# A cross network on one core: the first layer's second half column-tiled, its remainder transposed by DMA

## The chip, the cores and the metric

The kernel runs on one core of a Trainium2 chip. The metric is the device time of one execution in microseconds; lower is better. Before the change it is 131.33 us, the median of 3 runs (131.24 to 131.58).

## The reference

```python
B, F, D, L = 4096, 26, 16, 6
Din = min(F * D, 1024)                 # 416
# x0: (4096, 416), ws: (6, 416, 416), bs: (6, 416), all bf16
def reference(x0, ws, bs):
    x = x0
    for l in range(ws.shape[0]):
        x = x0 * (x @ ws[l] + bs[l]) + x
    return x
```

Six layers, each a product of 4096 rows with a 416 x 416 matrix, a bias, a multiplication with the first input and an addition.

## The kernel before, in words

The width of 416 is 3 x 128 + 32: three main blocks (`NK`) and a remainder of 32 (`R`). Through the first five layers the data lie transposed, features on the partitions. `XM` holds the three main blocks of all 4096 rows of the batch. `XR` holds the remainder, four groups of 512 rows stacked on the partitions, 32 partitions each. The batch is cut into two halves `s` of 2048 rows, each half into four quarters `g` of 512 rows (`CW`). A quarter of a half is written (s, g) here.

There are three shapes of product on the matmul engine (PE). A full product uses the array's 128 x 128 (L214 in the first layer, L327 in the last). A column-tiled group is four products of 128 x 32 that fill the array together (`mm_full`, L181; the remainder's, L193 and L198). A row-tiled group is four products of 32 x 128, the remainder's rows into the main blocks (L187, L221, L333).

The PSUM pool has four tiles of two banks under one tag, so every new tile waits for the release of an older one. ACT adds the bias and moves PSUM to SBUF (L165, L173). DVE multiplies by x0 and adds x (L166, L169, L174, L175).

The first layer (`first_layer(s)`) runs as the input arrives. SP issues a transposing load for each quarter (`load_x0t`, L76): four for half 0, (1,0), then `xrem` (the remainder columns of half 1, in rows, L85), then (1,1) to (1,3), then the weights of later layers (`load_wm`, `load_wr`), the rows of x0 for the last layer (`X0rows`) and the last bias. GpSimd (POOL) rearranges `xrem` into `xrig[:, 1]` (L134), between two fills of the block weights `WD` (`fill_wd`, L131). PE transposes four tiles of `xrig` with the identity (`x0_rem`, L157), for half 0 among its products, for half 1 at the end of half 0; DVE copies the result into `XR[0]` and, with the two halves of the partitions exchanged, into `XRd` (L160). `XRd` is the source of the row tiles of block 1 (L221).

Within a half the products are: the first two quarters for each block m into `pa[m]` (`full`), the row tiles of these and of `pb[0]`, the last two quarters into `pb[m]`, the row tiles of `pb[1]` and `pb[2]`, and the remainder's products (`mm_rem`, 16 products in four groups) into `pr`. Then follow the bias and the elementwise work for `pb` and `pr`.

Layers 1 to 4 run in the column-tiled shape, with the remainder of both halves in one `rem_pair`. The last layer turns the product round, so that rows of the batch come out on the partitions (`mm_q_full`, L327, 416 columns): eight blocks of 128 rows a round, in four rounds. Its elementwise work ends the kernel.

`tc.keep_in_program_order` pins an instruction behind those before it on its engine; the others the scheduler may move.

Of the kernel before, what the change touches and what calls it, by code (L numbers as in the profile page):

```python
# [11 lines left out]
BF16 = mybir.dt.bfloat16  # L12
FP32 = mybir.dt.float32
# [3 lines left out]
def kernel(  # L17
# [7 lines left out]
    nc = tc.nc  # L25
    B, D = x0.shape
    L = ws.shape[0]
    P = 128
    NK = 3
# [38 lines left out]
    def col0(s, g):  # L68
        return SW * s + CW * g

    def load_wm(eng, l):
        eng.dma_start(WM[:, l], ws[l, 0:NK * P, :].rearrange("(k p) n -> p k n", p=P))

    def load_x0t(s, g):
        c0 = col0(s, g)
        nc.sync.dma_start_transpose(out=XM[0][:, :, c0:c0 + CW], in_=x0[c0:c0 + CW, 0:NK * P])  # L76
# [35 lines left out]
            nc.gpsimd.tensor_copy(dst, src)  # L112
    for g in range(2, NG):
        load_x0t(0, g)
    load_x0t(1, 0)
    load_xrem1()
    for g in range(1, NG):
        load_x0t(1, g)
    load_wm(nc.sync, 1)
    for g in range(NG):  # L120
        load_wr(nc.sync, g, 1, L)
# [7 lines left out]
    def fill_wd(l0, l1):  # L129
        for g in range(NG):  # L130
            nc.gpsimd.tensor_copy(WD[32 * g:32 * g + 32, l0:l1, g, :], WR[32 * g:32 * g + 32, l0:l1, NK * P:D])  # L131

    fill_wd(0, 1)
    nc.gpsimd.tensor_copy(xrig[:, 1].rearrange("p i (g r) -> p i g r", g=NG), xrem[:].rearrange("p (g i) r -> p i g r", g=NG))  # L134
    fill_wd(1, L)

    wps = psum.tile([P, CW], FP32, tag="ps", name="wps")

# [7 lines left out]
    def bias_setup():  # L146
        pb = psum.tile([P, 4, 8], BF16, tag="ps", name="pb")
        for m in range(NK):
            nc.tensor.transpose(pb[:, m, 0:L], bsb[0:L, 128 * m:128 * m + 128], ident[0:L, 0:L])
        for g in range(NG):  # L150
            nc.tensor.transpose(pb[32 * g:32 * g + 32, 3, 0:L], bsb[0:L, NK * P:D], ident[0:L, 0:L], tile_position=(0, 32 * g))  # L151
        nc.vector.tensor_copy(bM[:], pb[:, 0:NK, 0:L])  # L152
        nc.vector.tensor_copy(bR[:], pb[:, 3, 0:L])

    def x0_rem(s, tpr):
        for i in range(4):
            nc.tensor.transpose(tpr[:, 128 * i:128 * i + 128], xrig[:, s, i, :], ident[:])  # L157
        for dst, src in ((slice(0, P), slice(0, P)), (slice(64, P), slice(0, 64)), (slice(0, 64), slice(64, P))):
            to = XR[0] if dst == src else XRd
            nc.vector.tensor_copy(to[dst, CW * s:CW * s + CW], tpr[src])  # L160

    def ew_main(l, s, m, h, pt, cur, nxt, pin=False):
        c0 = col0(s, 2 * h)
        t = tpool.tile([P, 2 * CW], BF16, name="t")
        nc.scalar.activation(t[:], pt[:].rearrange("p a b -> p (a b)"), ACT.Identity, bias=bM[:, m, l:l + 1], scale=1.0)  # L165
        prod = nc.vector.tensor_tensor(out=t[:], in0=t[:], in1=XM[0][:, m, c0:c0 + 2 * CW], op=ALU.mult)  # L166
        if pin:
            tc.keep_in_program_order(prod)
        nc.vector.tensor_tensor(out=nxt[:, m, c0:c0 + 2 * CW], in0=t[:], in1=cur[:, m, c0:c0 + 2 * CW], op=ALU.add)  # L169

    def ew_rem(l, s, pr, curR, nxtR):
        tr = tpool.tile([P, 2 * CW], BF16, name="t")
        nc.scalar.activation(tr[:, 0:CW], pr, ACT.Identity, bias=bR[:, l:l + 1], scale=1.0)  # L173
        nc.vector.tensor_tensor(out=tr[:, 0:CW], in0=tr[:, 0:CW], in1=XR[0][:, CW * s:CW * s + CW], op=ALU.mult)  # L174
        nc.vector.tensor_tensor(out=nxtR[:, CW * s:CW * s + CW], in0=tr[:, 0:CW], in1=curR[:, CW * s:CW * s + CW], op=ALU.add)  # L175
# [15 lines left out]
    def mm_rem(l, s, pr, cur, curR):  # L191
        for g in range(NG):
            nc.tensor.matmul(pr[32 * g:32 * g + 32, :], lhsT=WD[:, l, g, :], rhs=curR[:, CW * s:CW * s + CW],  # L193
                             start=True, stop=False, tile_position=(0, 32 * g))
        for k in range(NK):
            for g in range(NG):
                c0 = col0(s, g)
                nc.tensor.matmul(pr[32 * g:32 * g + 32, :], lhsT=WM[:, l, k, NK * P:D], rhs=cur[:, k, c0:c0 + CW],  # L198
                      start=False, stop=(k == NK - 1), tile_position=(0, 32 * g))
# [4 lines left out]
    def xl_dmat(s, k, nxt):  # L204
        nc.sync.dma_start_transpose(out=XLrows[:, 16 * s:16 * s + 16, 128 * k:128 * k + 128],
                                    in_=nxt[:, k, SW * s:SW * s + SW])

    def first_layer(s):
        cur, curR, nxt, nxtR = XM[0], XR[0], XM[1], XR[1]

        def full(pt, m, h, gl, after_row):
            c0 = col0(s, 2 * h + gl)
            for k in range(NK):
                nc.tensor.matmul(pt[:, gl, :], lhsT=WM[:, 0, k, 128 * m:128 * m + 128], rhs=cur[:, k, c0:c0 + CW],  # L214
                                 start=(k == 0 and not after_row), stop=(k == NK - 1 and after_row))

        def row(pt, m, h, opens):
            for gl in range(2):
                rg = 32 * ((2 * h + gl) ^ (2 if m == 1 else 0))
                src = XRd if m == 1 else curR  # L220
                nc.tensor.matmul(pt[:, gl, :], lhsT=WR[rg:rg + 32, 0, 128 * m:128 * m + 128],  # L221
                                 rhs=src[rg:rg + 32, CW * s:CW * s + CW],
                                 start=opens, stop=not opens, tile_position=(rg, 0))

        def ph(m):
            return psum.tile([P, 2, CW], FP32, tag="ps", name=f"ph{m}")

        pa = [ph(m) for m in range(NK)]
        if s == 0:
            for m in range(NK):  # L230
                full(pa[m], m, 0, 0, False)
            tp0 = psum.tile([P, CW], BF16, tag="ps", name="tpr")
            x0_rem(0, tp0[:])
            for m in range(NK):
                full(pa[m], m, 0, 1, False)
        else:
            for m in range(NK):
                for gl in range(2):
                    full(pa[m], m, 0, gl, False)
        pb = [ph(0)]  # L240
        row(pa[0], 0, 0, False)
        row(pb[0], 0, 1, True)
        row(pa[2], 2, 0, False)
        row(pa[1], 1, 0, False)
        for m in range(NK):
            ew_main(0, s, m, 0, pa[m], cur, nxt)
        for m in range(NK):
            if m:
                pb.append(ph(m))
            for gl in range(2):  # L250
                full(pb[m], m, 1, gl, m == 0)
        row(pb[1], 1, 1, False)
        row(pb[2], 2, 1, False)
        pr = psum.tile([P, 2, CW], FP32, tag="ps", name="pr")
        mm_rem(0, s, pr[:, 0, :], cur, curR)
        if s == 0:
            x0_rem(1, pr[:, 1, :].bitcast(BF16)[:, 0:CW])
        for m in range(NK):
            ew_main(0, s, m, 1, pb[m], cur, nxt, pin=(s == 0))
        ew_rem(0, s, pr[:, 0, :], curR, nxtR)  # L260

    bias_setup()
    pe_filler(1, CW)
    for s in range(NS):
        first_layer(s)

    def rem_pair(l, cur, curR, nxtR, feeds_last):
        pr2 = psum.tile([P, 2, CW], FP32, tag="ps", name="pr2")
        for s in range(NS):
            mm_rem(l, s, pr2[:, s, :], cur, curR)  # L270
        for s in range(NS):
            ew_rem(l, s, pr2[:, s, :], curR, nxtR)
            if feeds_last:
                nc.sync.dma_start_transpose(out=scrR[s][:], in_=nxtR[:, CW * s:CW * s + CW])

    def xl_rem(s):
        tc.keep_in_program_order(
# [42 lines left out]
    def q_cols(q, g):  # L320
        s, i = quads[q]
        c = col0(s, g) + 128 * i
        return slice(c, c + 128)

    def mm_q_full(q, g, py, closes):
        for k in range(NK):
            nc.tensor.matmul(py[:, 0:D], lhsT=cur[:, k, q_cols(q, g)], rhs=WM[:, l, k, :],  # L327
                             start=((not closes) and k == 0), stop=(closes and k == NK - 1))

# [33 lines left out]
    for q, at, done in rounds:  # L363
        tiles = [psum.tile([P, 2, CW], FP32, tag="ps", name=f"py{n}") for n in range(4)]
        bank = [tiles[n][:, a, :] for n, a in at]

        def close(u, n):
            tl, a = at[u]
            ew(q + u // 4, u % 4, n, tiles[tl][:, a:a + n, 0:D], nc.scalar if q + 2 == NQ and u == 7 else nc.sync)

        for u in range(done):
            mm_q_full(q, u, bank[u], False)
        mm_q_rem(q, bank[0:4], done)
        close(0, done)
        mm_q_rem(q + 1, bank[4:8], 0)
        for u in range(done, 8):
            mm_q_full(q + u // 4, u % 4, bank[u], True)
            if at is not PAIRS:
                close(u, 1)
            elif u % 2:  # L380
                close(u - 1, 2)
# [31 lines left out]
```

## Time and profile before

| | |
|---|---|
| median of 3 runs | 131.33 us (131.24 to 131.58) |
| the profiled execution | 130.71 us |
| its span | 128.9 us |
| PE busy | 123.1 us (96%) |
| DVE busy | 107.1 us (83%) |
| ACT busy | 86.9 us (67%) |
| mean DMA rate | 127 GB/s |
| PE's last wait for an input load ends | 12.14 us |
| first product of layer 1 (L181) | 26.73 us |
| first product of the last layer (L327) | 103.78 us |

Every time of a profile is counted from the span's start. The profiled execution is one of its own, beside the three timed ones; what lies between its time and its span is outside the program's instructions. The records of matmuls overlap: a column-tiled group shows four of 379 ns each. How long a stream really takes is read from the starts, or from the chain of work that ended last, not from the sum of its records.

### The profile page before, as it was taken

What the parts mean: (1) busy time and instruction counts of PE and PEld (TensorE: products, weight loads), DVE (VectorE), ACT (ScalarE), POOL (GpSimd) and SP (SyncE); (2) the same over time, 40 slices, a digit from 0 to 9 for tenths busy, and PEclk for the clock granted to TensorE, in tenths of its full rate; (3) what the DMA queues carried; (4) which work ended last, traced back from release to release, by engine and by line L of the source; (5) the groups of instructions that cost most, each with busy time, mean ns of one, the idle gap of its engine ahead of it and who ended that gap; (6) DMA issues with size and microseconds to landing.
All of it is one profiled execution on the core that took longest, in us unless ns stands there. A gap on an engine that the chain in (4) does not pass through costs nothing.

```text
span 128.9 us, 3973 instructions
## 1 busy us (share of the span) xinstructions
PE 123.1 (96%) x1690; PEld 54.9 (43%) x1690; DVE 107.1 (83%) x197; ACT 86.9 (67%) x99; POOL 5.9 (5%) x18
## 2 busy tenths in 40 slices
PE   6999999999999999999999999999999999999960
PEld 2343443354444444444444444444444445445420
DVE  1032979999999898989898989898989899898991
ACT  0426783987848577848668848668847896569670
POOL 4022200600000000000000000000000000000000
PEclk9999999999999999999999999999999999999999
DMA  3999999999990000000000000000297999995754
GB/s 106 237 203 217 170 158 260 247 328 333 336 299 11 5 0 8 0 0 5 0 5 0 5 0 5 0 5 0 42 166 164 123 219 178 187 323 188 231 179 139
DMA packets 42102, 16.37 MB, mean 127 GB/s; under 512 B 30906, under 2 KB 42084, under 8 KB 42084
## 3 DMA queue, kind: packets, MB, share of 16 engines
q1 hardware_dynamic: 39416, 15.56, 54.6%
q10 hardware_dynamic: 2668, 0.56, 2.3%
q8 instruction: 13, 0.21, 0.7%
q14 instruction: 5, 0.04, 0.1%
HBM read 6.15 MB, written 3.41 MB: 74 GB/s over the span
## 4 chain that ended last, share of the span: by engine, by line
PE 80%; DMA 8%; DVE 5%; issue 2%; SPq 1%; ACT 1%; DVEq 0%
PE pt L181 49%; PE ph L214 9%; DMA XM<-in_x_dram 8%; PE py L327 8%; PE pt L187 5%; PE pr L198 5%; DVE t L355 3%; DVE o L344 2%; PE pr L193 2%; SPq L76 1%; PE py L333 1%; PE ph L221 1%; PE py L336 1%; ACT t L354 1%; PE pr L157 0%
## 5 line engine op out<-in xcount | busy, mean ns | idle before, releaser
L181 PE MATMUL pt<-XM,WM 128*32 128x512 bf16 x1152 | 65.2, 379 | 0.0
L165 ACT ACTIVATE t<-pt,bM 128x1024 bf16<-128x1024 f32 x48 | 49.6, 1115 | 18.3 <-PE pt L187 18.3
L166 DVE TENSOR_TENSOR t<-t,XM 128x1024 bf16<-128x1024 bf16 x60 | 41.4, 690 | 5.3 <-ACT t L165 5.3
L169 DVE TENSOR_TENSOR XM<-t,XM 128x1024 bf16<-128x1024 bf16 x60 | 41.8, 696 | 3.4
L181 PEld LDWEIGHTS <-WM 128*32 128x32 bf16 x1152 | 29.7, 97 | 33.8 <-issue 5.1
L354 ACT CAST t<-py 128x416 bf16<-128x416 f32 (+1 forms) x23 | 14.8, 642 | 4.8 <-PE py L327 2.1
L327 PE MATMUL py<-WM,XM 128*128 128x416 bf16 x96 | 17.7, 340 | 0.0
L214 PE MATMUL ph<-XM,WM 128*128 128x512 bf16 x72 | 16.5, 379 | 0.1
L165 ACT ACTIVATE t<-ph,bM 128x1024 bf16<-128x1024 f32 x12 | 12.5, 1114 | 4.4 <-PE ph L221 4.4
L327 PEld LDWEIGHTS <-XM 128*128 128x128 bf16 x96 | 9.0, 98 | 8.5 <-issue 1.4
L355 DVE TENSOR_TENSOR t<-t,X0rows 128x416 bf16<-128x416 bf16 (+1 forms) x23 | 10.4, 454 | 1.2 <-ACT t L354 1.2
L214 PEld LDWEIGHTS <-WM 128*128 128x128 bf16 x72 | 6.8, 98 | 8.6 <-issue 1.3
L344 DVE TENSOR_TENSOR o<-t,XLrows 128x416 bf16<-128x416 bf16 (+1 forms) x23 | 10.3, 451 | 0.0
L173 ACT ACTIVATE t<-pr,bR 128x512 bf16<-128x512 f32 x10 | 6.4, 684 | 2.7 <-PE pr L198 2.1
L198 PE MATMUL pr<-XM,WM 128*32 128x512 bf16 x120 | 8.2, 379 | 0.0
L187 PE MATMUL pt<-XR,WR 32*128 32x512 bf16 x96 | 7.3, 379 | 0.0
L141 PE MATMUL wps<-warm 128*128 128x512 bf16 (+1 forms) x11 | 4.4, 593 | 1.2 <-DVE warm L94 1.2
L175 DVE TENSOR_TENSOR XR<-t,XR 128x512 bf16<-128x512 bf16 x10 | 4.2, 423 | 0.7
L198 PEld LDWEIGHTS <-WM 128*32 128x32 bf16 x120 | 3.2, 97 | 3.1
L106 ACT ACT_TABLE_LOAD x1 | 1.3, 1283 | 4.3 <-DMA WM<-in_ws_dram 4.3
L174 DVE TENSOR_TENSOR t<-t,XR 128x512 bf16<-128x512 bf16 x10 | 4.2, 418 | 0.0
L152 DVE CAST bM<-pb 128x18 f32<-128x18 bf16 x1 | 0.2, 177 | 4.6 <-PE pb L151 4.6
(39 smaller groups left out, 33.6 us busy)
## 6 DMA issues: line engine op xcount, KB each, us to landing
X0rows<-in_x_dram SPq DMA_DIRECT2D x4, 832.0 KB, 11.6
out_dram<-o SPq DMA_DIRECT2D x9, 208.0 KB, 2.4
WM<-in_ws_dram SPq DMA_DIRECT2D x5, 312.0 KB
out_dram<-o SPq DMA_DIRECT2D x13, 104.0 KB, 1.7
WR<-in_ws_dram SPq DMA_DIRECT2D x4, 130.0 KB, 4.1
WM<-in_ws_dram ACTq DMA_DIRECT2D x1, 312.0 KB
XM<-in_x_dram SPq DMA_TRANSPOSE x8, 4.9
xrig<-in_x_dram ACTq DMA_DIRECT2D x4, 32.0 KB, 4.1
```

Of the source, the lines that this page charges most:

```text
L165: nc.scalar.activation(t[:], pt[:].rearrange("p a b -> p (a b)"), ACT.Identity, bias=bM[:, m, l:l + 1], scale=1.0)
L166: prod = nc.vector.tensor_tensor(out=t[:], in0=t[:], in1=XM[0][:, m, c0:c0 + 2 * CW], op=ALU.mult)
L169: nc.vector.tensor_tensor(out=nxt[:, m, c0:c0 + 2 * CW], in0=t[:], in1=cur[:, m, c0:c0 + 2 * CW], op=ALU.add)
L173: nc.scalar.activation(tr[:, 0:CW], pr, ACT.Identity, bias=bR[:, l:l + 1], scale=1.0)
L181: nc.tensor.matmul(pts[g // 2][32 * q:32 * q + 32, g % 2, :], lhsT=WM[:, l, k, 128 * m + 32 * q:128 * m + 32 * q + 32], rhs=cur[:, k, c0:c ...
L187: nc.tensor.matmul(pts[g // 2][:, g % 2, :], lhsT=WR[32 * g:32 * g + 32, l, 128 * m:128 * m + 128], rhs=curR[32 * g:32 * g + 32, CW * s:CW ...
L198: nc.tensor.matmul(pr[32 * g:32 * g + 32, :], lhsT=WM[:, l, k, NK * P:D], rhs=cur[:, k, c0:c0 + CW], start=False, stop=(k == NK - 1), tile ...
L214: nc.tensor.matmul(pt[:, gl, :], lhsT=WM[:, 0, k, 128 * m:128 * m + 128], rhs=cur[:, k, c0:c0 + CW], start=(k == 0 and not after_row), sto ...
L327: nc.tensor.matmul(py[:, 0:D], lhsT=cur[:, k, q_cols(q, g)], rhs=WM[:, l, k, :], start=((not closes) and k == 0), stop=(closes and k == NK ...
L344: tc.keep_in_program_order(nc.vector.tensor_tensor(out=o, in0=t, in1=xl, op=ALU.add))
L354: nc.scalar.copy(tv, src)
L355: tc.keep_in_program_order(nc.vector.tensor_tensor(out=tv, in0=tv, in1=X0rows[:, b, :], op=ALU.mult))
```

## The change

- `xrem` is loaded ahead of (1,0). GpSimd's copy into `xrig[:, 1]` is issued ahead of all `fill_wd`. A transposing DMA from SBUF writes `XR[0]` of half 1 from `xrig[:, 1]`; on SP's queue it stands between (1,2) and (1,3). PE's four transposes for half 1 and DVE's copy into `XR[0]` go; the two copies into `XRd` read `XR[0]` now and are pinned.
- In half 1 of the first layer `full` calls `mm_full`, the column-tiled shape.
- The remainder's products of both halves are made by one `rem_pair`, in half 1, behind the last two quarters of block 0. The elementwise work for half 0's `pb` is issued in half 1, behind block 0's first two quarters (`late`), and pinned, with the two copies into `XRd` ahead of its third.
- In the last layer the first two blocks of the first round are made of column-tiled products (`split`).

```diff
--- before.py
+++ after.py
@@ -112,10 +112,13 @@
             nc.gpsimd.tensor_copy(dst, src)
     for g in range(2, NG):
         load_x0t(0, g)
-    load_x0t(1, 0)
     load_xrem1()
-    for g in range(1, NG):
+    for g in range(NG - 1):
         load_x0t(1, g)
+    nc.gpsimd.tensor_copy(xrig[:, 1].rearrange("p i (g r) -> p i g r", g=NG), xrem[:].rearrange("p (g i) r -> p i g r", g=NG))
+    nc.sync.dma_start_transpose(out=XR[0][:, CW:2 * CW].rearrange("p (i c) -> p i c", i=4),
+                                in_=xrig[:, 1].rearrange("p i c -> p (i c)"))
+    load_x0t(1, NG - 1)
     load_wm(nc.sync, 1)
     for g in range(NG):
         load_wr(nc.sync, g, 1, L)
@@ -130,9 +133,8 @@
         for g in range(NG):
             nc.gpsimd.tensor_copy(WD[32 * g:32 * g + 32, l0:l1, g, :], WR[32 * g:32 * g + 32, l0:l1, NK * P:D])
 
-    fill_wd(0, 1)
-    nc.gpsimd.tensor_copy(xrig[:, 1].rearrange("p i (g r) -> p i g r", g=NG), xrem[:].rearrange("p (g i) r -> p i g r", g=NG))
-    fill_wd(1, L)
+    for l0, l1 in ((0, 1), (1, L)):
+        fill_wd(l0, l1)
 
     wps = psum.tile([P, CW], FP32, tag="ps", name="wps")
 
@@ -152,12 +154,18 @@
         nc.vector.tensor_copy(bM[:], pb[:, 0:NK, 0:L])
         nc.vector.tensor_copy(bR[:], pb[:, 3, 0:L])
 
-    def x0_rem(s, tpr):
+    HALVES = ((slice(64, P), slice(0, 64)), (slice(0, 64), slice(64, P)))
+
+    def x0_rem0(tpr):
         for i in range(4):
-            nc.tensor.transpose(tpr[:, 128 * i:128 * i + 128], xrig[:, s, i, :], ident[:])
-        for dst, src in ((slice(0, P), slice(0, P)), (slice(64, P), slice(0, 64)), (slice(0, 64), slice(64, P))):
-            to = XR[0] if dst == src else XRd
-            nc.vector.tensor_copy(to[dst, CW * s:CW * s + CW], tpr[src])
+            nc.tensor.transpose(tpr[:, 128 * i:128 * i + 128], xrig[:, 0, i, :], ident[:])
+        nc.vector.tensor_copy(XR[0][:, 0:CW], tpr)
+        for dst, src in HALVES:
+            nc.vector.tensor_copy(XRd[dst, 0:CW], tpr[src])
+
+    def x0_rem1():
+        for dst, src in HALVES:
+            tc.keep_in_program_order(nc.vector.tensor_copy(XRd[dst, CW:2 * CW], XR[0][src, CW:2 * CW]))
 
     def ew_main(l, s, m, h, pt, cur, nxt, pin=False):
         c0 = col0(s, 2 * h)
@@ -205,10 +213,22 @@
         nc.sync.dma_start_transpose(out=XLrows[:, 16 * s:16 * s + 16, 128 * k:128 * k + 128],
                                     in_=nxt[:, k, SW * s:SW * s + SW])
 
+    def rem_pair(l, cur, curR, nxtR, feeds_last):
+        pr2 = psum.tile([P, 2, CW], FP32, tag="ps", name="pr2")
+        for s in range(NS):
+            mm_rem(l, s, pr2[:, s, :], cur, curR)
+        for s in range(NS):
+            ew_rem(l, s, pr2[:, s, :], curR, nxtR)
+            if feeds_last:
+                nc.sync.dma_start_transpose(out=scrR[s][:], in_=nxtR[:, CW * s:CW * s + CW])
+
     def first_layer(s):
         cur, curR, nxt, nxtR = XM[0], XR[0], XM[1], XR[1]
 
         def full(pt, m, h, gl, after_row):
+            if s == 1:
+                mm_full(0, s, m, 2 * h + gl, {h: pt}, cur, not after_row, after_row)
+                return
             c0 = col0(s, 2 * h + gl)
             for k in range(NK):
                 nc.tensor.matmul(pt[:, gl, :], lhsT=WM[:, 0, k, 128 * m:128 * m + 128], rhs=cur[:, k, c0:c0 + CW],
@@ -230,13 +250,18 @@
             for m in range(NK):
                 full(pa[m], m, 0, 0, False)
             tp0 = psum.tile([P, CW], BF16, tag="ps", name="tpr")
-            x0_rem(0, tp0[:])
+            x0_rem0(tp0[:])
             for m in range(NK):
                 full(pa[m], m, 0, 1, False)
         else:
             for m in range(NK):
                 for gl in range(2):
                     full(pa[m], m, 0, gl, False)
+                if m == 0:
+                    for mm in range(NK):
+                        if mm == 2:
+                            x0_rem1()
+                        ew_main(0, 0, mm, 1, late[mm], cur, nxt, pin=True)
         pb = [ph(0)]
         row(pa[0], 0, 0, False)
         row(pb[0], 0, 1, True)
@@ -249,29 +274,21 @@
                 pb.append(ph(m))
             for gl in range(2):
                 full(pb[m], m, 1, gl, m == 0)
+            if s == 1 and m == 0:
+                rem_pair(0, cur, curR, nxtR, False)
         row(pb[1], 1, 1, False)
         row(pb[2], 2, 1, False)
-        pr = psum.tile([P, 2, CW], FP32, tag="ps", name="pr")
-        mm_rem(0, s, pr[:, 0, :], cur, curR)
         if s == 0:
-            x0_rem(1, pr[:, 1, :].bitcast(BF16)[:, 0:CW])
+            late.extend(pb)
+            return
         for m in range(NK):
-            ew_main(0, s, m, 1, pb[m], cur, nxt, pin=(s == 0))
-        ew_rem(0, s, pr[:, 0, :], curR, nxtR)
-
+            ew_main(0, s, m, 1, pb[m], cur, nxt)
+
+    late = []
     bias_setup()
     pe_filler(1, CW)
     for s in range(NS):
         first_layer(s)
-
-    def rem_pair(l, cur, curR, nxtR, feeds_last):
-        pr2 = psum.tile([P, 2, CW], FP32, tag="ps", name="pr2")
-        for s in range(NS):
-            mm_rem(l, s, pr2[:, s, :], cur, curR)
-        for s in range(NS):
-            ew_rem(l, s, pr2[:, s, :], curR, nxtR)
-            if feeds_last:
-                nc.sync.dma_start_transpose(out=scrR[s][:], in_=nxtR[:, CW * s:CW * s + CW])
 
     def xl_rem(s):
         tc.keep_in_program_order(
@@ -322,8 +339,14 @@
         c = col0(s, g) + 128 * i
         return slice(c, c + 128)
 
-    def mm_q_full(q, g, py, closes):
+    def mm_q_full(q, g, py, closes, split=False):
         for k in range(NK):
+            if split:
+                c0 = q_cols(q, g).start
+                for r in range(4):
+                    nc.tensor.matmul(py[32 * r:32 * r + 32, 0:D], lhsT=cur[:, k, c0 + 32 * r:c0 + 32 * r + 32], rhs=WM[:, l, k, :],
+                                     start=((not closes) and k == 0), stop=(closes and k == NK - 1), tile_position=(0, 32 * r))
+                continue
             nc.tensor.matmul(py[:, 0:D], lhsT=cur[:, k, q_cols(q, g)], rhs=WM[:, l, k, :],
                              start=((not closes) and k == 0), stop=(closes and k == NK - 1))
 
@@ -369,7 +392,7 @@
             ew(q + u // 4, u % 4, n, tiles[tl][:, a:a + n, 0:D], nc.scalar if q + 2 == NQ and u == 7 else nc.sync)
 
         for u in range(done):
-            mm_q_full(q, u, bank[u], False)
+            mm_q_full(q, u, bank[u], False, split=(q == 0))
         mm_q_rem(q, bank[0:4], done)
         close(0, done)
         mm_q_rem(q + 1, bank[4:8], 0)
```

## The prediction

> **What bounds the kernel now.** First the page's busy shares (busy us, share of the span, instructions) and its chain that ended last.
>
> ```profile
> PE 123.1 (96%) x1690; PEld 54.9 (43%) x1690; DVE 107.1 (83%) x197; ACT 86.9 (67%) x99; POOL 5.9 (5%) x18
> ...
> PE 80%; DMA 8%; DVE 5%; issue 2%; SPq 1%; ACT 1%; DVEq 0%
> ```
>
> The matmul engine bounds it: from 12.14 us to the last products there is no gap on PE, and the 8% of DMA is the load that PE waits for until 12.14. So a change has to shorten PE's stream, and pays for every wait that it puts in.
>
> Next the chain in order of time (start us, us, what). It prices a product and a change of array shape.
>
> ```profile
> 17.18 3.88 PE ph L214 x18
> 21.06 0.54 PE ph L221 x8
> 21.61 3.99 PE ph L214 x18
> ...
> 26.90 2.59 PE pt L181 x48
> ...
> 30.03 2.71 PE pt L181 x48
> ...
> 103.85 1.16 PE py L327 x6
> ```
>
> 18 full products of 512 columns take 3.88 us, 0.216 each. 48 column-tiled ones are 12 groups of four in 2.59 us, 0.216 a group. So column tiling by itself gains nothing. What costs is the change between shapes: the same 18 after the row-tiled products (L221) take 3.99, the same 48 after row tiles (L187) 2.71, about 0.11 more. The six at 103.85 are the first full ones after column tiles: 1.16 against 6 x 0.175 = 1.05 (24 take 4.33 later, less one switch).
>
> Then the timeline of the first layer (start us, us, engine, line, tiles).
>
> ```profile
> 15.80 0.40 PE L193 MATMUL pr<-XR,WD 128*32 128x512 bf16 x4
> ...
> 16.78 0.40 PE L157 MATMUL pr<-ident,xrig 128*128 128x128 bf16 x4
> ...
> 17.01 4.05 PE L214 MATMUL ph<-XM,WM 128*128 128x512 bf16 x18
> ...
> 21.00 0.60 PE L221 MATMUL ph<-XR,WR 32*128 32x512 bf16 x6
> ...
> 21.54 4.06 PE L214 MATMUL ph<-XM,WM 128*128 128x512 bf16 x18
> ...
> 26.73 2.76 PE L181 MATMUL pt<-XM,WM 128*32 128x512 bf16 x48
> ```
>
> The second half's products start at 17.01, its row tiles at 21.00, its second part at 21.54, the next layer at 26.73.
>
> Last SP's queue in the timeline: the loads that this stretch eats.
>
> ```profile
> 7.10 3.69 SPq L76 DMA_TRANSPOSE XM<-in_x_dram  x2
> 10.83 0.58 SPq L85 DMA_DIRECT2D xrem<-in_x_dram  x1
> 11.45 6.47 SPq L76 DMA_TRANSPOSE XM<-in_x_dram  x3
> 17.97 1.35 SPq L72 DMA_DIRECT2D WM<-in_ws_dram  x1
> ```
>
> These transposing loads are limited by the DMA engines. The trace's packet records, cut at 1536 packets a load, show them back to back: (1,0) runs 10.77 to 13.03, xrem 12.77 to 14.07, (1,1) 14.03 to 15.96, (1,2) 15.96 to 17.90, (1,3) 17.91 to 20.71. Their semaphores are complete at 13.95, 15.14, 17.13, 19.93 and 21.27. The last load is long because one 16 KB instruction fetch holds a DMA engine for 1.10 us at 17.84. PE first uses the four quarters at 17.01, 17.66, 21.54 and 22.20 (the second and the fourth three products after the first and the third), so the margins are 3.1, 0.5, 1.6 and 0.9 us. No wait shows, but this stretch runs close behind its loads.
>
> **The change, part by part.**
>
> *PE, first layer.* Out of the gap between the halves go 16 remainder products and four transposes, 15.80 to 17.01: 1.21 us. The second half then starts at 15.80. The 16 products come back behind its fourth quarter, and those of the second half join them there: a pair costs 0.21 + 0.65 + 0.22 + 0.65 = 1.73 us (the chain at 32.74). At the end 26.73 - 25.85 = 0.88 falls away. Without waits: quarter 0 at 15.80, quarter 1 at 16.45, row tiles at 15.80 + (21.00 - 17.01) = 19.79, quarter 2 at 20.33, quarter 3 at 20.98. From there to the next layer: 0.65 for that quarter, 1.73, 12 groups 2.59, then 0.10 to the row tiles and 0.33 past them, 5.40 in all: 26.38 instead of 26.73, that is -0.35. The same by counting: four transposes (0.22) and one of seven switches (0.11) go.
>
> *PE, last layer.* The first two blocks become column-tiled, and the switch at 103.85 goes: -0.10. The switch to the row tiles behind them stays. Nothing hides PE here: at 115.81 ACT, and then DVE to the end, still start from PE's product, so this and any earlier shift arrives at the end whole. Together -0.45.
>
> *A mechanism against column tiles.* They need four weight loads for one. If these went one after another, 97 ns each (L181), a group would last 4 x 97 = 388 ns and not 216, and 36 groups would cost 6.2 us: near 137. The 1152 loads at L181 keep 0.216 a group, like the full ones at L214 (98 ns a load), so I cost it at nothing. The Trainium skill, TensorEngine Tiling (Array Packing), Restrictions and Gotcha 2, says that column tiling rules out the array's fast weight load, which speaks for that mechanism; the trace shows no price for it.
>
> *xrem ahead of (1,0).* The order of equal data changes, not its sum: xrem's 1.2 us of packets then end near 12.0, (1,0)'s at 14.03, and with its 0.92 from last packet to semaphore (1,0) lands near 14.9, still ahead of 15.80. (1,1) and (1,2) keep their place, about 17.13 and 19.93. Here is the first new wait: quarter 1 is wanted at 16.45, 1.21 earlier than before (17.66), and its load is not. PE waits 0.68 (bounds: 0, if it lands in the shortest time after its last packet that a load here shows, 0.56 after 15.96; and 1.2, if it slips by half of another load). That eats the earlier start.
>
> *GpSimd's copy and the new transpose.* xrem lands 1.07 behind its last packet as before, near 13.1; the copy takes 0.79 (L134), so at about 14.0 the source is there; SP reaches the transpose at about 15.9, behind (1,2), and should not wait. It stands ahead of (1,3) and everything behind that on SP's queue. The nearest row is the transpose of the same shape:
>
> ```profile
> L274 SPq DMA_TRANSPOSE scrR<-XR x2: 1217/1221/1225, 97.5 to 98.8; - x2
> ```
>
> It holds SP for 1.22 us; its 512 packets move in 0.6 us, a third of a load's. So (1,3) comes later by 0.6 (if the DMA engines set the pace, as they do here) to 1.27 (if SP's issue does), or not at all if a gap is filled. I take 0.65, since the packets run back to back: 21.27 + 0.65 = 21.92. PE wants quarter 3 at 20.98 + 0.68 = 21.66, so another 0.30 goes, semaphore included: it starts at 21.96, the next layer at 27.36. That is +0.63, and with the last layer's -0.10, +0.53.
>
> *What else is behind that queue.* WM of layer 1 lands at 22.36 and is wanted at 26.7; the remainder weights land by 25.1 and are wanted at 29.4; X0rows at 40 for use at 107. All of them can come 1.3 later. fill_wd for layer 0 now stands behind GpSimd's copy, to 15.0; it is wanted near 23.
>
> *DVE and ACT.* DVE loses one 0.42 copy; the two XRd copies now read SBUF (0.27, the memset of 256 columns, to 0.42, as from PSUM) and are pinned ahead of the last late product, so behind them wait that product and the next half's. The transposed remainder should land 0.6 to 1.3 behind its last packet near 18.6, 19.2 to 19.9, ahead of the row tiles at 20.5. DVE ends the layer near 31.5 (ACT hands over the last two tiles near 28.4 and 29.4, 1.33 us each on DVE, one still queued); the next layer's remainder pair wants it at 27.36 + 5.8 = 33.2. ACT frees the pair's PSUM at about 22.0 (row tiles at 20.5, 0.4 for them, 1.1 for L165); it is wanted at 21.96 + 0.65 = 22.6. I cost these at nothing; the cover is 0.6 us for PSUM and 1.7 for DVE, and once it is gone each us costs one.
>
> **Sum.** The profiled execution took 130.71 us, 128.9 of it span, 1.8 around it; the median of the three runs is 131.33, 0.6 above. -0.35 - 0.10 + 0.68 + 0.30 = +0.53 on the median: 131.9.
>
> **The rivals.**
> 1. *No load is late*: -0.45, 130.9. It needs (1,1) by 16.45 and (1,3) by 20.98. For it: the load hit by the fetch would take 1.9 instead of 2.8, and semaphores follow the last packet by 0.56 to 2.0, which may turn out lower. Against: both land later than that already before, without the transpose.
> 2. *Only quarter 1 is late*, and the transpose hides in the delay that the fetch makes anyway: -0.45 + 0.68, 131.6, within the bound.
> 3. *The row tiles wait for the transposed remainder*: if it lands behind the fetch near 21.3, the two copies and the second set of row tiles follow it; quarter 3 then starts at 21.3 + 0.7 + 0.33 + 0.65 = 23.0, the next layer at 28.4, +1.57 in all, 132.9. It decides once the landing is past about 20.3. For it: (1,2), just ahead on the same queue, lands 2.0 behind its last packet. Against: there is little data.
> 4. *Column tiles load their weights one after another*: 36 x 0.172 more, near 137; against it every column-tiled row of this trace.
>
> **Chances.** Forecast 0.38; rivals 0.24, 0.22, 0.12 and 0.02; other waits (PSUM, DVE) 0.02. What a measurement of this kernel can tell from no change is about 0.3%, 0.39 us. Faster is rival 1, 0.24; within it rival 2, 0.22; slower the rest, 0.54. The range takes in rivals 1, 2 and 3, from 130.85 to 132.9; beyond it lie rival 4 and later landings still.
>
> **What would show it.** PE: second half at 15.8 with an idle gap of about 0.7 ahead of its second quarter, laid to XM's load; another of about 0.3 ahead of the fourth; the next layer near 27.4; no L157 in the second half; the first products of the last layer with no 0.11 ahead of them. SP: the new transpose issued at about 15.9 for 1.2 us, (1,3) landing near 21.9. The forecast is wrong if PE has no gap between 15.8 and the next layer, or if the long gap is ahead of the row tiles.

## The result and the profile after

The change makes the kernel slower: 132.49 us (median of 6, 132.1 to 132.85) against 131.22 (median of 6), ratio 1.0112, 95% interval 1.0082 to 1.0142. A later set gave 132.31 against 130.97, ratio 1.0097 (1.0067 to 1.0127). The forecast was 131.9, slower.

The profiled execution of the kernel after took 132.58 us, its span is 130.8; before it was 130.71 and 128.9. The two profiles lie 1.87 apart and the medians 1.27, so the profiles show the loss somewhat too large.

The page of the kernel after, busy shares and the chain:

```profile
PE 123.2 (94%) x1812; PEld 55.9 (43%) x1812; DVE 107.1 (82%) x196; ACT 86.7 (66%) x99; POOL 6.6 (5%) x18
...
PE 73%; SPq 8%; DMA 8%; DVE 5%; issue 2%; ACT 1%; DVEq 0%
```

PE is as busy as before, in a span 1.9 us longer, and its share of the chain falls from 80% to 73%; SP's queue takes 8% where it had 1%. The time went into waits for loads. The timeline of PE in the first layer of the kernel after shows where (its lines have moved: L189 is the column-tiled product that was L181, L241 the row tile that was L221):

```profile
15.95 0.83 PE L189 MATMUL ph<-XM,WM 128*32 128x512 bf16 x12
18.16 3.42 PE L189 MATMUL ph<-XM,WM 128*32 128x512 bf16 x60 [1.38 <-DMA XM<-in_x_dram]
21.80 0.61 PE L241 MATMUL ph<-XR,WR 32*128 32x512 bf16 x6 [0.22 <-DMA XR<-xrig]
...
22.44 1.57 PE L189 MATMUL ph<-XM,WM 128*32 128x512 bf16 x24
...
28.59 0.61 PE L189 MATMUL pt<-XM,WM 128*32 128x512 bf16 x8
```

Half 1 starts at 15.95, 1.06 earlier than before (17.01). After quarter 0 of the first block, 0.65 us, PE stands until quarter 1 has landed. The row tiles would follow at 18.16 + 15 x 0.216 + 0.10 = 21.50; they start at 21.80, when the transposed remainder is there. Layer 1 starts at 28.59 instead of 26.73. In SP's queue the new transpose stands where it was foreseen, 0.8 us later than forecast (15.9):

```profile
16.73 1.30 SPq L119 DMA_TRANSPOSE XR<-xrig  x1
...
18.08 1.50 SPq L76 DMA_TRANSPOSE XM<-in_x_dram  x1
```

By the trace's semaphore counts the four quarters land at 15.77, 18.12, 19.60 and 23.14, the remainder at 21.76. The last layer's gain is in the chain: its first products stand with 1.05 (24 column-tiled ones) where six full ones had 1.16.

```profile
105.72 1.05 PE py L347 x24
```

### The profile page after: what moved, and what is told of

The parts are those of the page before. It is cut to its first block, busy times and chain, and to the rows that moved or that the text cites. A ratio compares the mean times of both kernels' runs of the same rounds, so it can differ in the third digit from the quotient of the medians.

```text
span 130.8 us, 4218 instructions
## 1 busy us (share of the span) xinstructions
PE 123.2 (94%) x1812; PEld 55.9 (43%) x1812; DVE 107.1 (82%) x196; ACT 86.7 (66%) x99; POOL 6.6 (5%) x18
## 4 chain that ended last, share of the span: by engine, by line
PE 73%; SPq 8%; DMA 8%; DVE 5%; issue 2%; ACT 1%; DVEq 0%
PE pt L189 49%; SPq L76 8%; PE py L350 7%; PE pt L195 5%; PE pr L206 5%; DMA XM<-in_x_dram 4%; DMA XR<-xrig 4%; DVE t L378 3%; PE ph L189 3%; DVE o L367 2%; PE pr L201 2%; PE py L356 1%; PE py L347 1%; PE ph L241 1%; PE py L359 1%
## 5 line engine op out<-in xcount | busy, mean ns | idle before, releaser
L189 PE MATMUL pt<-XM,WM 128*32 128x512 bf16 x1152 | 65.2, 380 | 0.0
L189 PEld LDWEIGHTS <-WM 128*32 128x32 bf16 x1296 | 33.7, 97 | 39.0 <-issue 7.4
L350 PE MATMUL py<-WM,XM 128*128 128x416 bf16 x90 | 16.5, 340 | 0.0
L350 PEld LDWEIGHTS <-XM 128*128 128x128 bf16 x90 | 8.5, 98 | 7.8 <-issue 1.4
L189 PE MATMUL ph<-XM,WM 128*32 128x512 bf16 x144 | 8.6, 380 | 1.4 <-DMA XM<-in_x_dram 1.4
L234 PE MATMUL ph<-XM,WM 128*128 128x512 bf16 x36 | 8.4, 380 | 0.0
L181 ACT ACTIVATE t<-pr,bR 128x512 bf16<-128x512 f32 x10 | 6.3, 684 | 2.6 <-PE pr L206 2.6
L234 PEld LDWEIGHTS <-WM 128*128 128x128 bf16 x36 | 3.3, 97 | 4.3 <-issue 0.8
L206 PEld LDWEIGHTS <-WM 128*32 128x32 bf16 x120 | 3.3, 97 | 3.2
L134 POOL COPY WD<-WR 32x32 bf16<-32x32 bf16 (+1 forms) x8 | 4.0, 498 | 10.5 <-DMA WR<-in_ws_dram 10.1
```

Of the source, the lines that this page charges most:

```text
L189: nc.tensor.matmul(pts[g // 2][32 * q:32 * q + 32, g % 2, :], lhsT=WM[:, l, k, 128 * m + 32 * q:128 * m + 32 * q + 32], rhs=cur[:, k, c0:c ...
```

## The experiments

Theory A: PE's stream is 0.45 us shorter, and the whole loss is PE waiting for half 1's loads and the transposed remainder. Theory B: the loss is in the column tiles, the order of PSUM tiles, or the moved and pinned elementwise work. Each set ran beside the kernel before on its chip; the ratios are against that. Times in the first expectations go by the first chip, where before took 131.22; in the later sets before took 130.68 to 130.97. The kernel after itself ran a second time only in the set of e5, v1 and v2, on one chip with them.

**e1_no_waits: PE waits for nothing in half 1.**

```diff
-                mm_full(0, s, m, 2 * h + gl, {h: pt}, cur, not after_row, after_row)
+                mm_full(0, 0, m, 2 * h + gl, {h: pt}, cur, not after_row, after_row)
...
-                c0 = col0(s, g)
+                c0 = col0(s if l else 0, g)
...
-                                 rhs=src[rg:rg + 32, CW * s:CW * s + CW],
+                                 rhs=src[rg:rg + 32, 0:CW],
```

> The kernel after, with the second half's products in the first layer (main blocks, row tiles and remainder columns) reading the first half's data, which landed long before; all loads, the new transpose and every instruction stay, only what PE reads differs (so the values of half 1 are not the reference's). Theory A (the stream of products is 0.45 us shorter and all of the loss is PE waiting for half 1's loads and for the transposed remainder): no idle time on PE between 15.9 and layer 1, layer 1 at 26.5 instead of 28.59, time 130.8, 0.45 below before. Theory B (the loss is in the column tiles, the PSUM order or the moved and pinned elementwise work): stays near 132.5.

Measured: 130.35 us against 130.68, ratio 0.9970 (0.9957 to 0.9983), faster than before. Its timeline of PE:

```profile
15.94 4.07 PE L189 MATMUL ph<-XM,WM 128*32 128x512 bf16 x72
19.94 0.60 PE L241 MATMUL ph<-XR,WR 32*128 32x512 bf16 x6
...
20.48 1.48 PE L189 MATMUL ph<-XM,WM 128*32 128x512 bf16 x24
...
26.53 2.77 PE L189 MATMUL pt<-XM,WM 128*32 128x512 bf16 x48
```

One run of 72 column-tiled products with no gap, row tiles 4.00 later, layer 1 at 26.53: from half 1's start 10.59 us, the prediction's working has 10.58 (15.80 to 26.38). Every instruction of the change is in this kernel, in the same order on every engine; only what PE reads differs, so most of half 1's values are computed from half 0's data. Theory B falls.

**e2_no_quarters and e3_no_remainder: one of the two waits taken away.** e2 has the first two edits of e1, e3 the third.

> The kernel after, with the main-block and remainder products of the second half reading the first half's quarters (so PE never waits for the four quarters of half 1), the row tiles still reading the transposed remainder. Theory A: the row tiles are reached at 19.9 and wait for the remainder, which landed at 21.76 in the profile after; so nearly the whole loss comes back at that place: row tiles at 21.5 to 21.8, time 132.2 to 132.5. Rival A2 (the quarters alone are the cause, the remainder is in time once PE does not crowd it): 130.8.

> The kernel after, with only the row tiles of the second half reading the first half's remainder, so that they never wait for the new transpose; the quarters of half 1 are awaited as after. Theory A: PE waits for quarter 1 until 18.1 (1.5 us lost) as after, nothing at the row tiles, and then for quarter 3 until 23.1 instead of 22.7: time 132.2 to 132.5, no gain by it. Rival A3 (the transposed remainder is the cause, as rival 3 of the prediction has it): 131.2 or less.

Measured: e2 131.44 us, ratio 1.0059 (1.0044 to 1.0074); e3 131.63, ratio 1.0077 (1.0062 to 1.0092). Neither rival holds. Theory A's times are 1.0 to 1.3 us above its before of 131.22; measured are 0.76 and 0.95 above 130.68. Timelines of PE, e2 and then e3:

```profile
15.74 4.07 PE L189 MATMUL ph<-XM,WM 128*32 128x512 bf16 x72
20.73 0.61 PE L241 MATMUL ph<-XR,WR 32*128 32x512 bf16 x6 [0.92 <-DMA XR<-xrig]
```

```profile
17.35 3.42 PE L189 MATMUL ph<-XM,WM 128*32 128x512 bf16 x60 [1.01 <-DMA XM<-in_x_dram]
20.70 0.60 PE L241 MATMUL ph<-XR,WR 32*128 32x512 bf16 x6
...
22.26 0.83 PE L189 MATMUL ph<-XM,WM 128*32 128x512 bf16 x12 [0.18 <-DMA XM<-in_x_dram]
```

In e2 the wait moves to the row tiles, in e3 it stays at quarter 1 and a new one shows at quarter 3. In each, PE goes on 0.04 to 0.05 us behind the landing (20.68, 17.31, 22.22), as theory A has it. Its miss lies in the landings, which were earlier in these profiles than in that of the kernel after (remainder 20.68 instead of 21.76, quarter 1 17.31 instead of 18.12).

Against the kernel after (1.0104, the mean of its two ratios, from other chips) the one gains 0.45%, the other 0.27%, both together 1.34%. The 0.27% alone is within the intervals. So a good part of the waits lies one behind the other: what one gives back, the next one takes.

**e4_gap_filled: half 0's remainder products back between the halves.**

```diff
         if s == 0:
-            late.extend(pb)
+            pr0 = psum.tile([P, 2, CW], FP32, tag="ps", name="pr")
+            mm_rem(0, 0, pr0[:, 0, :], cur, curR)
+            late.extend(pb + [pr0])
             return
...
-                rem_pair(0, cur, curR, nxtR, False)
+                pr1 = psum.tile([P, 2, CW], FP32, tag="ps", name="pr")
+                mm_rem(0, 1, pr1[:, 0, :], cur, curR)
+                ew_rem(0, 1, pr1[:, 0, :], curR, nxtR)
```

(Half 0's `ew_rem` follows the three late `ew_main`.)

> The kernel after, with the remainder products of half 0 back between the halves (own PSUM tile) and those of half 1 alone behind the fourth quarter; transpose by DMA, load order and column tiles stay. Theory A: the 0.86 us of products run in a gap that PE spends waiting for quarter 1, so the row tiles start as after (21.5 to 21.8) and the rest is 0.86 shorter: layer 1 at 27.7, time 131.6. Theory B (loads do not matter): as after, 132.5, since the work is the same.

Measured: 130.88 us, ratio 1.0012 (0.9995 to 1.0028): no loss clear of noise is left (0.2 us; theory A had 0.4 above before). Timeline of PE:

```profile
16.61 0.82 PE L189 MATMUL ph<-XM,WM 128*32 128x512 bf16 x12
17.60 3.42 PE L189 MATMUL ph<-XM,WM 128*32 128x512 bf16 x60 [0.16 <-DMA XM<-in_x_dram]
20.97 0.61 PE L241 MATMUL ph<-XR,WR 32*128 32x512 bf16 x6
...
26.81 0.61 PE L189 MATMUL pt<-XM,WM 128*32 128x512 bf16 x8
```

The same work, 0.86 us of it done in time that the kernel after spends waiting. The loads were earlier too (quarter 1 at 17.56), on another chip than the kernel after's. But v1 and v2 below, which have this edit and a new order of the quarters, ran beside the kernel after on one chip and take 1.2 to 1.3 us less. So this edit carries most of the loss.

**e5_no_transpose: e3 without the transposing DMA.**

```diff
-    nc.sync.dma_start_transpose(out=XR[0][:, CW:2 * CW].rearrange("p (i c) -> p i c", i=4),
-                                in_=xrig[:, 1].rearrange("p i c -> p (i c)"))
...
+        nc.gpsimd.tensor_copy(XR[0][:, CW:2 * CW], XR[0][:, 0:CW])
```

> The kernel whose row tiles read the first half's remainder, now also without the transposing DMA on SP's queue (the remainder of half 1 is filled by a GpSimd copy of half 0's instead, so half 1's remainder is left out of the result). What the transpose costs the loads behind it: theory A says 0.65 to 1.3 us on the fourth quarter, which then lands near 21.2 instead of 22.2 and is no longer awaited (wanted near 21.9); 0.3 us less than with the transpose, about 0.6 above before, all of it quarter 1. Rival: the transpose is free on the queue; the fourth quarter still lands at 22.2 and the time stays 0.9 above before.

> The kernel after, unchanged, beside the variants of this set on one chip. The two half-relieved kernels (quarters not awaited, remainder not awaited) were 0.8 to 0.9 above before, so theory A (waits in parallel, each hidden behind the other) has it at 0.9 to 1.3 above before. If it is under 0.9, the half-relieved kernels gained nothing at all.

Measured: the kernel after 132.31 (ratio 1.0097), 1.34 above before, just past the expected 0.9 to 1.3; e5 132.00, ratio 1.0070 (1.0039 to 1.0101), as e3 with the transpose in. Quarter 3 lands at 23.15. That looks like the rival, but does not settle it: in this profile the 16 KB instruction fetch comes at 20.76, in the middle of quarter 3, and not in the transpose.

The price can be read from pairs of profiles in which the fetch meets the same load. From the landing of quarter 1 to that of quarter 3 it is 4.14 us before and 4.16 in e7_order_alone, both without the transpose; with it 4.63, 4.66, 4.64 and 4.60 (e1, e2, e4, v1). In all six the fetch comes before (1,2) has landed. So the transpose costs the load behind it about 0.5 us; the prediction had 0.65.

**v1_quarters_first and v2_transpose_earlier: can it be mended?** Both build on e4.

```diff
-            for m in range(NK):
-                for gl in range(2):
+            for gl in range(2):
+                for m in range(NK):
                     full(pa[m], m, 0, gl, False)
-                if m == 0:
+                if gl == 0:
```

v2 also issues the transpose behind (1,1) instead of (1,2).

> The variant with the gap filled by half 0's remainder products, and half 1's first two quarters in the order quarter 0 for all three blocks, then quarter 1, so that quarter 1 is wanted 1.3 us later. Theory A: the 0.3 us wait for quarter 1 goes, but the row tiles then wait for the transposed remainder (20.9) as long: within 0.1 of the variant with the gap filled, 0.1 to 0.2 above before. If only quarter 1 mattered: 0.1 to 0.2 below before.

> As v1_quarters_first, and the transposing DMA is issued behind (1,1) instead of behind (1,2). Theory A: the remainder lands before 19.5 and the row tiles wait for nothing; the last load is not earlier (22.2), is wanted at 21.9, and from it to layer 1 are 4.5 us of products: layer 1 at 26.7, within 0.15 of before. Rival: the instruction fetch meets another load and one of the two last ones is 1 us late: 0.5 to 1 above before.

Measured: v1 131.01 us, ratio 0.9991 (0.9963 to 1.0019); v2 131.08, ratio 1.0008 (0.9986 to 1.0031). No difference from before, as expected. In v1 the wait moves to the row tiles:

```profile
16.92 4.17 PE L189 MATMUL ph<-XM,WM 128*32 128x512 bf16 x72
21.59 0.61 PE L241 MATMUL ph<-XR,WR 32*128 32x512 bf16 x6 [0.50 <-DMA XR<-xrig]
```

In this profile quarter 1 (18.22) and the remainder (21.55) land as late as in the kernel after, and layer 1 still starts 1.16 us earlier (27.43): what was mended is the work in front of the waits, not the loads. In v2 the row tiles wait for nothing, and the last quarter is what is late; the 24 products from 21.64 take 1.72 us, 1.48 where nothing is awaited (e1):

```profile
16.98 4.18 PE L190 MATMUL ph<-XM,WM 128*32 128x512 bf16 x72
21.09 0.60 PE L242 MATMUL ph<-XR,WR 32*128 32x512 bf16 x6
...
21.64 1.72 PE L190 MATMUL ph<-XM,WM 128*32 128x512 bf16 x24
...
27.06 0.61 PE L190 MATMUL pt<-XM,WM 128*32 128x512 bf16 x8
```

The last load sets the end of this stretch: 22.48 plus 4.5 us of products.

**e6_fetch_later, v3_full_quarters, v4_fewer_fillers: the instruction fetch.** e6 keeps half 1's first two quarters in full products, v3 adds the order of v1, v4 leaves out 5 warming products.

```diff
-            if s == 1:
+            if s == 1 and h == 1:
                 mm_full(0, s, m, 2 * h + gl, {h: pt}, cur, not after_row, after_row)
...
-    pe_filler(8, CW)
+    pe_filler(3, CW)
```

> The kernel after, with half 1's first two quarters as full products again (36 instructions fewer per 18 products times three, 108 in all; the same number of shape changes, the same product time), the last two quarters column-tiled. The 16 KB instruction fetch of PE came in each profile when PE had about 236 instructions behind it in column tiles (193 in the full products of before); with 108 fewer it should come only at the row tiles or behind them, after 21.5 us. Theory A (the fetch on one DMA engine holds the transposing load that it meets by 1 to 1.7 us): the remainder lands near 20.0 instead of 21.6, the fourth quarter near 21.4 instead of 23.0, PE still waits for quarter 1 until 18.1 and for nothing else: layer 1 at 28.0 instead of 28.5, 0.5 us less than after, 0.8 above before. Rival F (the fetch does not matter, the queue is just slow): remainder at 21.6, as after, 1.3 above before.

> As e6_fetch_later, and half 1's first two quarters in the order quarter 0 for all blocks, then quarter 1. Theory A: quarter 1 is wanted at 17.9 and lands at 17.3 to 18.1, so up to 0.2 us; the row tiles start at 20.1 to 20.3, just behind the remainder (20.0); the fetch then comes at about 20.5 and meets the fourth quarter, which lands at 22.5 to 23.0 instead of 21.4 and is wanted at 21.4: 1.1 to 1.6 us lost there, 0.7 to 1.2 above before. If the fetch stays behind the fourth quarter: 0.1 to 0.4 below before. Rival F: as after.

> As v3_full_quarters, with 5 of the 11 warming products at the start left out (10 instructions), so that the fetch comes 0.3 to 0.5 us later, about 21.0. Theory A: the fourth quarter has fewer packets left when the fetch comes: lands 21.5 to 23.0, between 0.4 below and 1.0 above before. If the warming products were needed, PE's granted clock or the first products' rate drops and the first half is later (row tiles of half 0 behind 15.7).

Measured: e6 132.48, ratio 1.0125 (1.0101 to 1.0148); v3 132.37, ratio 1.0119 (1.0089 to 1.0149); v4 132.43, ratio 1.0112 (1.0053 to 1.0171). These are 1.65 to 1.76 us above before; 0.8 was expected of e6, 0.7 to 1.2 of v3. In e6 and v3 the fetch did not move as expected: with fewer instructions it came at 19.11 and 18.67, with 165 and 175 instructions started instead of 236, and met the transpose again (landed at 21.25 and 20.80).

Layer 1 starts earlier than in the kernel after (28.12 and 27.65 instead of 28.59), but 0.3 to 0.4 us are lost later: from there to the end e6, v3 and v4 take 102.5 to 102.6 us, all other runs 102.1 to 102.2. A later fetch, at 100.18 in e6, meets the small transpose `scrR`, which brings the remainder into the last layer. It lands 2.05 to 2.11 us behind the load ahead of it in these three, 0.40 to 0.66 in all others, and ACT waits for it (1.1 us in the kernel after). The wait in e6, and its chain in the last layer, which goes through ACT to PE:

```profile
ACT XLrows L295 <- DMA scrR<-XR: 1.7, 1, 1.7
...
105.85 1.13 ACT t L173
106.98 0.04 issue
107.03 0.35 PE py L356 x2
```

So these times do not tell what column tiles cost. The streams do: after the wait for quarter 1, e6 makes 15 full products in 3.40 us where the kernel after makes 60 column-tiled ones in 3.42.

```profile
17.71 3.40 PE L234 MATMUL ph<-XM,WM 128*128 128x512 bf16 x15 [0.94 <-DMA XM<-in_x_dram]
```

Column tiles have no part in the loss. The Trainium skill, TensorEngine Tiling (Array Packing), Restrictions, has column tiles without fast weight load; here too no price for it shows.

In v4 the fetch came at 22.72, behind all of half 1's loads, and PE waited for none of them. But half 0 was 1.5 us late, since without those products the first ones run at half speed (4.00 us for nine, 2.12 in the kernel after); the rest of its loss is the 0.3 us in the last layer. The chain of v4:

```profile
5.99 4.00 PE ph L234 x9
9.98 0.43 PE tpr L161 x4
10.41 2.30 PE ph L234 x9
```

From quarter 1's landing to that of the remainder v4 has 2.73 us; with the fetch on (1,2) it is 3.33 to 3.39, with the fetch on the transpose 3.44 to 3.64. By this one profile without a fetch, it costs 0.6 to 0.9 us wherever in this chain it falls; at `scrR` it costs 1.4 to 1.7 (2.05 to 2.11 less 0.40 to 0.66). The Trainium skill, DMA: Bandwidth & Descriptors, Queues, rings and completion order, says that a DMA engine drains a whole packet before it turns to another queue; the trace has the fetch as one packet of 16 KB that takes 0.93 to 1.30 us, which fits, but it does not show what waited behind it on its engine.

**e7_order_alone: before, with xrem ahead of (1,0).**

```diff
-    load_x0t(1, 0)
     load_xrem1()
-    for g in range(1, NG):
+    for g in range(NG):
         load_x0t(1, g)
```

> The kernel before, with one edit: xrem is loaded ahead of (1,0) instead of behind it. What the order alone does to quarter 1. Theory A (the prediction's step: only the order of equal work changes): (1,0) lands near 15 and (1,1) where it did, 17.1 to 17.4; quarter 1 is wanted at 17.66, so no wait: within 0.1 us of before. Rival O (the small packets of xrem in front cost the chain of loads some 0.5 to 1 us): (1,1) at 17.6 to 18.1, up to 0.45 us of wait: 0.1 to 0.5 above before.

Measured: 130.64 us, ratio 0.9987 (0.9966 to 1.0008); quarter 0 lands at 15.00, quarter 1 at 17.30. The order costs nothing that shows, as theory A and the prediction had it.

## Why the prediction was right, and where its sizes were off

The way held, and the place of the first wait: half 1 starts early and stands before quarter 1. The size did not: the forecast has +0.53, the medians give +1.27 and +1.34. That the time lies in the range is owed to rival 3, which set its upper end. The terms, against the two profiles:

| step | predicted | profile after |
|---|---|---|
| PE's stream, first layer | -0.35 | -0.35 (e1: 10.59 from half 1's start, predicted 10.58) |
| half 1's start | 15.80 | 15.95, +0.15 |
| wait for quarter 1 | +0.68 | +1.56 (16.60 to 18.16) |
| row tiles, remainder | 0 | +0.30 |
| row tiles, the `XRd` copies | 0 | +0.10 (0.64 for the two sets instead of 0.54) |
| wait for quarter 3 | +0.30 | +0.08 |
| last layer | -0.10 | -0.11 |
| sum | +0.53 | +1.73 (spans: 1.9) |

Up to the last DVE instruction the two profiles differ by 1.77 (126.32 and 128.09), which the sum meets within 0.04. The last 0.10 of the spans lies between that instruction and the end, and no run explains it.

The rows follow PE's stream, and each holds only what the waits ahead of it have left. With the remainder at 21.76, PE would have stood before the row tiles until 21.80 with quarter 1 in time as well (from 15.95 + 4.00 = 19.95). So the chain of the kernel after, in both of its profiles, runs through the transposed remainder, not through quarter 1:

```profile
16.73 5.02 DMA XR<-xrig
21.80 0.71 PE ph L241 x8
```

This is rival 3's path, which had a chance of 0.12. It put the remainder near 21.3 and layer 1 at 28.4; measured are 21.76 and 28.59.

The step that was mis-sized is quarter 1's wait. It took one profile's landing, 17.13, for the load's place. In the later profiles with xrem first it lands between 17.29 and 18.22, and before's 17.13 is earlier than all of them. The upper bound of that step, 1.2, was passed too. Neither the order of loads (e7: 17.30) nor the rest of the change (e2, e3, v3: 17.29 to 17.31) fixes it at 18.1; in the two profiles of the kernel after half 0 was later as well (its last row tiles at 15.63 and 15.65, 15.18 in e3). The chip may have a part: where the kernel after ran its second time, four profiles have quarter 1 at 17.44 to 18.22, the four of e1 to e4, on another chip, at 17.29 to 17.61. No run separates chip and kernel, so what makes it late there stays open. Whether this scatter reaches the times is not shown either: e5's ten runs spread over 1.0 us and e1's over 0.35, but before itself spreads over 1.56 on e5's chip (28 runs) and 0.69 on e1's (19).

The second step that failed is "I cost these at nothing" for the remainder. It was to land at 19.2 to 19.9; it landed at 20.47 to 21.76 where it stood behind (1,2). The fetch was put on the load behind it, (1,3), and in the kernel after it meets the transpose itself. Already the reading of before had it one load too late: of (1,2)'s 16 semaphore counts four come at 18.50 to 18.71 and twelve at 19.80 to 19.93, so the fetch, 17.84 to 18.94, falls into (1,2). Rival 3's condition, a landing past 20.3, is met. In the table it adds only 0.4, since quarter 1 had made PE later already; with quarter 1 out of the way, it cost 0.9 (e2).

The rest stands. Rival 1's price, -0.45, lies within e1's interval (0.22 to 0.56 below before; -0.33 by the medians); half 1's start, 0.14 later than assumed, would make up the difference. Rival 2 missed that there are three gates. Rival 4 has no case. The cover named for PSUM, DVE and the weights behind the queue was enough: e1 has no gap up to layer 1.

## What to carry to other kernels

Work that is moved out of a place where an engine does not wait may have been the reason that it does not. Before shortening a stream that runs close behind its loads, set each load's landing beside the time at which it would now be wanted; a saving ahead of a late load is worth nothing, and work that is moved behind it is paid in full. Gates that lie behind one another have to be taken away together in the experiment: one by one they gave back 0.45% and 0.27%, together 1.34%. Which gate ends last is read from the chain, not from the longest gap: the gap here stood before quarter 1, the chain ran through the remainder. And a landing read from one profile is one draw, so its margin needs several.

## What was not expected of the hardware

An instruction fetch, one 16 KB packet on one DMA engine, makes a transposing load that it meets complete late: in the kernel after 10 of the remainder's 16 semaphore counts come at 19.94 to 20.07 and six at 21.67 to 21.76, the fetch running from 19.88 to 20.89. Why six counts are late and not one, no run shows. That the fetches are PE's is inferred from their number: with 122 more products and as many more weight loads, the page of the kernel after has 14 on their queue instead of 13.

Without 5 of the 11 warming products the first nine full products took 4.00 us instead of 2.12, while the granted clock of that slice of the page still reads 9 tenths or more: that row does not show what slowed them.

DVE's copy of 64 x 512 bf16 from SBUF takes 0.288 us, the one from PSUM took 0.422.
